# Retention ahead of two mixtures of experts: POOL's mixes and stores of x pinned in the first block alone, and one joined tile of mixed x kept and stored one step later

## Chip, cores and metric

The kernel runs on one core of a Trainium2 chip. The metric is the device time of one execution in microseconds (us), before and after; smaller is better. TensorE (PE) multiplies matrices, VectorE (DVE), ScalarE (ACT) and GpSimd (POOL) work on elements, SyncE (SP) starts most transfers, and POOL starts the stores that this change touches.

## Reference

Three layers run one after the other on 2304 tokens of 512 features: retention (4 batches, 8 heads, 576 positions), a mixture of 4 experts that all run, and a mixture of 8 experts with routing.

```python
def _attn_ref(q, k, v):
    scores = scale * np.matmul(q, k.transpose(0, 1, 3, 2))
    Dmat = np.where(rel >= 0, gamma[:, None, None] ** rel[None, :, :], 0.0)
    return np.matmul(scores * Dmat[None], v)

def _moe_ref(x, domain_probs, w1, w2):
    p = domain_probs / (domain_probs.sum(-1, keepdims=True) + 1e-09)
    for e in range(E):
        out += p[:, e:e + 1] * (np.maximum(x @ w1[e], 0.0) @ w2[e])

def _moe2_ref(x, w_gate, w_output_gate, w1, w2):
    e_idx = np.argmax(x @ w_gate, axis=1)
    # each token through its own expert alone, scaled by its two gates
```

## The kernel before

**Stages.** Retention is cut into 36 steps of 64 positions (`NSTEP`, `NC` = 9 steps to a batch). Four steps (`NS`) make a block of 256 tokens, so there are nine blocks (`NB`). The first mixture starts as soon as the first block of x is there; the steps of the retention are then threaded between its matrix products: `at_hook()` runs one step at a time, at fixed places of the loops over blocks and experts. Steps 0 to 5 run ahead of that in program order. This interleaved stretch lasts until about 175 us of the span; from there on the first mixture goes on alone, and the second follows.

**One step.** `at_step(s)` has PE work out what the state adds (`at_past`, L300), the scores of the next step (`at_scores`, L277), the step's own part (`at_b`, L309) and the new state (`at_state`, L324). All of it lands in one PSUM tile `uo`, of which there is one after the opening. DVE masks the scores (`pf`, L282), adds the state (`sn`) and then reads x out of `uo` into the SBUF tile `xf` of the block (`at_x`, L358). Until it has done so, the next step's L300 cannot write `uo`. `at_parts` then splits the step's x into a high half (ACT, L365) and a low half (POOL, L366), in the tile `xo` (`xc` for blocks 0 and 1). POOL also scales the keys for the state (`ks`, L256), from a tile `vkr` that SP loads.

**Mixed x.** The first mixture multiplies large matrices by a scheme of seven products in place of eight, which needs sums of blocks of x. `x_mix(b, i)` makes them on POOL in place in `xf`, two subtractions at a time, four to a block (L373). `x_keep(b, i)` splits half of the mixed tile: ACT copies the high half (L384), POOL subtracts for the low one (L385). The results go to `xm`, or for blocks 0 and 1 to the upper half of `xc`. `x_store` then writes the tiles to DRAM (`xcd`) by a transfer that POOL starts (L390 and L392).

**Buffers.** `xf` has two buffers, so the first `at_x` of block b+2 (step 4b+8) waits until both keeps of block b have read theirs. `xo` has two. Before the change, mixed x of blocks 2 to 8 lies in two tiles, `xm0` and `xm1`, with one buffer each; a keep of the next block waits for the store of the same half.

**Order.** A scheduler places instructions on each engine. `tc.issue_after(...)` pins an instruction behind another on its own queue; `pace["pool"]` and `pace["act"]` hold the latest such instruction. By `ago(s, b)`, the steps since a block's last one, the kernel before mixes at 1 and 2, keeps at 3 and 4 and stores each half of mixed x at once, pinned.

**Weights.** ACT (L219, L220) and DVE (L221) split the experts' weights into high and low parts, and ACT L487 with DVE L488 mix them. These stand between the instructions of the steps on the same queues. The first mixture's second products are L711 (`po`), its first ones L559 (`ph`).

Of the kernel before, what the change touches and what calls it, by code (L numbers as in the profile page):

```python
# [10 lines left out]
F16 = mybir.dt.float16  # L11
# [12 lines left out]
NSTEP = B * NC  # L24
NT = N // 128
BT = 256
NB = N // BT
# [10 lines left out]
HB = BT // 2  # L38
# [5 lines left out]
BM = 5  # L44
# [100 lines left out]
def kernel(  # L145
# [19 lines left out]
    pe, act, dve, pool, sp = [InOrder(tc, e) for e in (nc.tensor, nc.scalar, nc.vector, nc.gpsimd, nc.sync)]  # L165
# [34 lines left out]
    xcd = dram.tile([NB * 128, 2, 8, 2, HB], F16, name="xcd")  # L200
# [27 lines left out]
    at_1 = at_ctx.enter_context(tc.tile_pool(name="at_1", bufs=3))  # L228
# [3 lines left out]
    qks, raws, pm, st, uos, pace = {}, {}, {}, {}, {}, {}  # L232
    xcs, xfs, xos = {}, {}, {}
# [5 lines left out]
    def load_qk(s):  # L239
        b, c = divmod(s, NC)  # L240
        a = at_raw.tile([128, 10, C], F32, name="qkr", bufs=4)
        pace["sp"] = sp.dma_start(out=a[:, 0:10 if c else 8], in_=qk[b, c][:, 0:10 if c else 8])
        qks[s] = a

    def load_vk(s):
        b, c = divmod(s, NC)
        t = at_raw.tile([128, 10, D], F32, name="vkr")
        pace["sp"] = sp.dma_start(out=t[:, 0:4 if c == NC - 1 else 10], in_=vk[b, c][:, 0:4 if c == NC - 1 else 10])
        raws[s] = (t,)

    def at_split(s):

        ks = None
        if s % NC < NC - 1:
            ks = at_1.tile([128, 4, D], F32, name="ks")
            pool.tensor_tensor(  # L256
                out=ks, in0=raws[s][0][:, 4:8], in1=cst("ktab", 4, 1).to_broadcast([128, 4, D]), op=ALU.mult
            )
        raws[s] += (ks,)
# [25 lines left out]
    def at_open(s):  # L285
        uos[s] = [at_ps[-1].tile([128, 2, 512], F32, tag="uo", name="uo"), set(), None]
# [88 lines left out]
    def x_keep(b, i):  # L375
        m = xfs[b]
        if xos[b][1] is None:
            xos[b][1] = [at_1.tile([128, 2, 2, 2, HB], F16, name="xm" + str(h), bufs=1) for h in range(2)]
        with tc.issue_after(pace["act"].ins):
            if isinstance(xos[b][1], list):  # L380
                hi, lo = [xos[b][1][i][:, a] for a in range(2)]
            else:
                hi, lo = [xos[b][1][:, a, 2 * i:2 * i + 2] for a in range(2)]
            act.activation(out=hi, in_=m[:, i], func=ACTF.Copy)  # L384
            pool.tensor_tensor(out=lo, in0=m[:, i], in1=hi, op=ALU.subtract)  # L385

    def x_store(b, i):
        dst = xcd[b * 128:(b + 1) * 128]
        if i < 2:
            pace["pool"] = pool.dma_start(out=dst[:, :, 4 * i:4 * i + 4], in_=xos[b][i])  # L390
        else:
            pace["pool"] = pool.dma_start(out=dst[:, :, 2 * i:2 * i + 2], in_=xos[b][1][i - 2])  # L392

    def at_step(s):

# [784 lines left out]
    def later_step(s):  # L1180
# [11 lines left out]
        out=p_sb, in0=p_sb, scalar=SO1, in1=ps_inv.to_broadcast([128, NT, E1]), op0=ALU.mult, op1=ALU.mult  # L1192
# [16 lines left out]
    pe, act, dve, pool, sp = nc.tensor, nc.scalar, nc.vector, nc.gpsimd, nc.sync  # L1209
# [4 lines left out]
    def others():  # L1214
        with tc.issue_after(pace["sp"].ins):
            sp.dma_start(out=wgr, in_=wg)
            sp.dma_start(out=kb, in_=cb)
            sp.dma_start(out=k16, in_=c16)

    def gate_split():  # L1220
        with tc.issue_after(pace["act"].ins), tc.issue_after(pace["dve"].ins):
            split(wgr, wg_sb[:, 0], wg_sb[:, 1], S_G)
# [9 lines left out]

    def at_hook():
        s = nxt[0]
        if s >= NSTEP + 4:
            return
        nxt[0] += 1
        if s + 4 < NSTEP:
            load_vk(s + 4)
        if s + 3 < NSTEP:  # L1240
            load_qk(s + 3)
        if NS + 2 < s < NSTEP - 2:
            at_split(s + 2)
        if s == 4 * NS:
            others()
        if s == 6 * NS:
            gate_split()
        if s == NS + 2:
            with tc.issue_after(pace["pe"].ins), tc.issue_after(pace["pool"].ins):
                at_split(s + 2)  # L1250
                at_open(s)
                at_scores(s)
                at_state(s, s, 4 * C)
                at_sum(s, s, 4 * C)
        for b in range(NB):
            if ago(s, b) == 1:
                with tc.issue_after(pace["pool"].ins):
                    x_mix(b, 0)
        if s < NSTEP:
            at_step(s)  # L1260
        for b in range(NB):
            n = ago(s, b)
            if n == 2:
                with tc.issue_after(pace["pool"].ins):
                    x_store(b, 0)
                x_mix(b, 1)
            if 2 < n < 5:
                x_keep(b, n - 3)
                if b > 1:
                    with tc.issue_after(pace["pool"].ins):  # L1270
                        x_store(b, n - 1)
            if b < 2 and n == 5:
                x_store(b, 1)
        if s == NSTEP + 3:
            at_ctx.close()
            wm["b"] = ctx.enter_context(tc.tile_pool(name="w_b", bufs=1)).tile([128, 6, 2048], F16, name="wm_b")
            later["raw"] = ctx.enter_context(tc.tile_pool(name="raw_s", bufs=3))
            later["s16"] = ctx.enter_context(tc.tile_pool(name="s16", bufs=4))
            later["pool"] = ctx.enter_context(tc.tile_pool(name="later", bufs=2))
            later["mix"] = mix_ctx.enter_context(tc.tile_pool(name="mix_ps", bufs=1, space=PSUM))  # L1280
# [107 lines left out]
    for e in range(E1):  # L1388
        for b in range(NB + (e == E1 - 1)):
            last = b == NB  # L1390
            if e == 0 and b <= BM:
                a = [lambda b=b, j=j: l1_first(b, j) for j in range(4)] if 0 < b < BM else l1_mixed(0, b) if b else []
                d = b - (b >= BM)
                c = [] if b == BM - 1 else [lambda d=d, i=i, h=h: l2(d, i, h) for h in range(2) for i in range(2)]
                units = a + c
                if b == BM:
                    units = [a[0], c[0], a[1], a[2], c[1], a[3], c[2], a[4], a[5], c[3], a[6]]
            else:
                a = [] if last else l1_mixed(e, b)
                c = l2_mixed(*prev) if prev else []  # L1400
                units = [f for n in range(7) for f in ([a[n]] if a else []) + ([c[n]] if c else [])]
            if (e, b) == (E1 - 1, 1):
                c_ctx.close()
                open_routing()
                gp.append(ctx.enter_context(tc.tile_pool(name="gp", bufs=2)))
            for u, unit in enumerate(units):
                unit()
                z_from(e == 0 and b < BM and (b == 0 or u >= 4))
                if e == 0:
                    if u == 1 and b >= 2 or (b, u) == (1, 5):  # L1410
                        with tc.issue_after(pace["sp"].ins):
                            x_load((b + 1) % NB, sp, base=b + 1 < BM)
                elif (e, b) == (1, 0):
                    if u == 0:
                        x_load(1, sp)
                elif u == 0 and not last and (e, b) != (E1 - 1, NB - 1):
                    with tc.issue_after(pace["pool"].ins):
                        x_load((b + 1) % NB, pool)
                if e == 0:
                    for _ in range(1 + (b == 0 and u % 2)):  # L1420
                        at_hook()
                if not last:
                    w_plan(e, b, u)
                    s_plan(e, b, u)
                if e == E1 - 1:
                    for g in gate_at.pop((b, u), ()):
                        g()
                    if gate:
                        gate.pop(0)()
            if e == E1 - 1:  # L1430
                if b:
                    gate_plan(b - 1)
                if b == NB - 1:
                    while s_at[0] <= n_stage + 2 or pend_store:
                        s_hook()
                    m_open_x()
                    lane_load(0, 1, early_row[0])
                    for s in range(EARLY):
                        m_x(s, early[5], s, TE * 128)
                if last:  # L1440
                    m_open()
            if e or b >= BM:
                prev = (e, b)
# [112 lines left out]
```

## Time and profile before

| | before |
|---|---|
| median of three runs | 1006.8 us (1004.93 to 1008.66) |
| profiled execution | 1005.25 us, span 1003.5 us |
| granted PE clock, mean | 0.994 of full |
| PE busy in the span | 961.8 us (96%) |
| weight loads, DVE, ACT, POOL busy | 826.3, 573.6, 535.6, 420.9 us |

The span reaches from the first to the last instruction; the execution's own time has 1.75 us more. PE's idle time is what a change of order can give back or add to. The page's row of 40 slices has PE below full only in the first seven (to about 175 us) and in the last one.

### The profile page before, as it was taken

Reading aid. Unit: us, or ns where it says so; the run is one execution under the profiler, and the core shown is the slowest. Engines: PE = TensorE matmul, PEld = TensorE weight load, DVE = VectorE, ACT = ScalarE, POOL = GpSimd, SP = SyncE. Lnnn points to the kernel's source line nnn. Section 1 sums busy time; section 2 is a strip of 40 time slices with the busy share of each in tenths; the row PEclk is TensorE's granted clock in tenths of the full one; section 3 lists DMA queues with packets and bytes.
Section 4 is the critical chain, followed back from the end, with each engine's and each line's share of the span. In section 5 each row is a group of like instructions: output and inputs, shape, how many; then the busy total and the mean of one; then the engine's idle time right before and its main releaser. Section 6 shows DMA issues by size and latency. Waiting matters only on the chain. (4 is left out here: it accounts for less than half of the span.)

```text
span 1003.5 us, 31925 instructions
## 1 busy us (share of the span) xinstructions
PE 961.8 (96%) x13507; PEld 826.3 (82%) x13507; DVE 573.6 (57%) x1290; ACT 535.6 (53%) x1019; POOL 420.9 (42%) x446
## 2 busy tenths in 40 slices
PE   6988899999999999999999999999999999999994
PEld 6565476899999999999999999999987677777773
DVE  5664472466767777766777676888888211211210
ACT  4354353567758777766777676676643122221211
POOL 4686665555546234555343464343223222112111
PEclk9999999999999999999999999999999999999998
DMA  9697875336466777556668726978835616554690
GB/s 351 215 352 236 289 242 183 115 101 200 153 197 177 250 266 235 174 184 198 220 195 297 272 71 160 264 211 227 230 121 203 232 43 229 217 205 158 256 391 32
DMA packets 96051, 209.48 MB, mean 209 GB/s; under 512 B 21598, under 2 KB 42334, under 8 KB 93600
## 3 DMA queue, kind: packets, MB, share of 16 engines
q1 hardware_dynamic: 82784, 159.20, 47.8%
q0 software_dynamic: 13120, 48.20, 15.0%
q8 instruction: 108, 1.77, 0.7%
q14 instruction: 39, 0.32, 0.1%
HBM read 197.88 MB, written 52.99 MB: 250 GB/s over the span
## 5 line engine op out<-in xcount | busy, mean ns | idle before, releaser
L672 PEld LDWEIGHTS <-op 128*128 128x128 f16 x2604 | 245.7, 98 | 26.0 <-POOL s L211 0.6
L606 POOL TENSOR_TENSOR op<-sm,op 128x512 f16<-128x512 f32 x124 | 142.3, 1158 | 226.2 <-ACT op L605 226.1
L587 PEld LDWEIGHTS <-wm_a 128*128 128x128 f16 x3264 | 192.9, 98 | 3.8
L587 PE MATMUL ph<-xc,wm_a 128*128 128x128 f16 x2112 | 132.2, 219 | 0.0
L605 ACT ACTIVATE op<-sm 128x512 f16<-128x512 f32 x124 | 77.5, 634 | 86.3 <-DVE sm L610 84.8
L1094 DVE SCALAR_TENSOR_TENSOR h_s<-p_h,h_s 128x512 f16<-128x512 f32 x40 | 27.6, 691 | 159.1 <-ACT h_s L1093 151.4
L1101 PE MATMUL p_y<-wm_a,h_s 128*128 128x512 f16 x480 | 107.2, 379 | 0.5 <-DVE h_s L1094 0.5
L672 PE MATMUL pv<-wm_a,op 128*128 128x256 f16 x792 | 97.4, 273 | 0.0
L672 PE MATMUL px<-wm_a,op 128*128 128x256 f16 x744 | 91.3, 272 | 0.7 <-DVE acc L680 0.7
L1101 PEld LDWEIGHTS <-h_s 128*128 128x128 f16 x480 | 46.6, 98 | 52.4 <-DVE h_s L1094 0.7
L221 DVE TENSOR_TENSOR s<-pz,s 128x512 f16<-128x512 f32 x111 | 73.9, 682 | 15.9 <-ACT s L220 15.9
L1104 POOL DMA_INDIRECT out_dram<-y_s,sidxm x17 | 17.3, 1019 | 146.3 <-ACT y_s L1103 137.7
L587 PEld LDWEIGHTS <-wm_b 128*128 128x128 f16 x1296 | 76.9, 98 | 1.4
L219 ACT ACTIVATE pz<-sr 128x512 f32<-128x512 f32 x111 | 65.6, 605 | 15.1 <-DVE rk L830 9.1
L490 POOL TENSOR_TENSOR wr<-wr 128x512 f32<-128x512 f32 x48 | 60.5, 1272 | 29.8 <-ACT pz L219 29.1
L1093 ACT ACTIVATE h_s<-p_h 128x512 f16<-128x512 f32 x40 | 23.9, 597 | 78.9 <-PE p_h L1084 74.9
L220 ACT ACTIVATE s<-pz 128x512 f16<-128x512 f32 x111 | 64.0, 599 | 0.6
L221 DVE TENSOR_TENSOR wm_a<-pz,wm_a 128x512 f16<-128x512 f32 x62 | 42.0, 688 | 37.7 <-ACT wm_a L220 37.3
L1103 ACT ACTIVATE y_s<-p_y,x_g 128x512 f32<-128x512 f32 x20 | 13.7, 687 | 92.8 <-PE p_y L1101 83.7
L680 DVE SCALAR_TENSOR_TENSOR acc<-px,p_sb,acc 128x256 f32<-128x256 f32 x124 | 59.1, 476 | 6.7 <-PE px L672 6.5
L1084 PEld LDWEIGHTS <-wm_b 128*128 128x128 f16 x1056 | 60.0, 98 | 2.8 <-issue 0.6
L1084 PE MATMUL p_h<-x_s,wm_b 128*128 128x128 f16 x1056 | 61.6, 219 | 0.3 <-issue 0.2
(231 smaller groups left out, 1809.4 us busy)
## 6 DMA issues: line engine op xcount, KB each, us to landing
wm_a<-w2d SPq DMA_DIRECT2D x20, 2048.0 KB, 8.8
wr<-in_w_dram SPq DMA_DIRECT2D x40, 512.0 KB, 7.9
wm_b<-w1d SPq DMA_DIRECT2D x10, 2048.0 KB
wm_a<-w1d SPq DMA_DIRECT2D x10, 2048.0 KB
sr<-in_w1s_dram SPq DMA_DIRECT2D x64, 256.0 KB, 4.3
w1d<-s SPq DMA_DIRECT2D x64, 256.0 KB, 4.9
sr<-in_w2s_dram SPq DMA_DIRECT2D x64, 256.0 KB, 5.0
w2d<-s SPq DMA_DIRECT2D x64, 256.0 KB, 5.2
```

What stands on the lines that cost most here:

```text
L219: act.activation(out=z, in_=raw, func=ACTF.Copy, scale=scale)
L220: act.activation(out=hi, in_=z, func=ACTF.Copy)
L221: dve.tensor_tensor(out=lo, in0=z, in1=hi, op=ALU.subtract)
L490: pace["pool"] = pool.tensor_tensor(out=quarter(e, n, k, to), in0=quarter(e, n, k, x), in1=quarter(e, n, k, y), op=op)
L587: pe.matmul(bank[:, i], lhsT=w[:, k, u, 128 * i:128 * i + 128], rhs=x[:, v, d, k], start=(first and i == 0 and n == 0), stop=(n == 5), ski ...
L605: act.activation(out=hi, in_=s, func=ACTF.Copy)
L606: pool.tensor_tensor(out=lo, in0=s, in1=hi, op=ALU.subtract)
L672: pe.matmul(out, lhsT=o[a][:, v, k], rhs=w[c][:, k, u], start=(first and n == 0), stop=(n == 11), skip_group_check=True,)
L680: step = dve.scalar_tensor_tensor(out=a, in0=src, scalar=p_sb[:, b * TB + i, e:e + 1], in1=a, op0=ALU.mult, op1=ALU.add)
L1084: pe.matmul(ph[:, j], lhsT=w[k][:, x, f * 128:(f + 1) * 128], rhs=xs[:, y, k], start=(n == 0), stop=(n == 3 * KD - 1),)
L1094: dve.scalar_tensor_tensor(out=lo, in0=ph, scalar=0.0, in1=hi, op0=ALU.max, op1=ALU.subtract)
L1101: pe.matmul(po, lhsT=h[:, a, k], rhs=w[k][:, b], start=(n == 0), stop=(n == 3 * KF - 1))
```

## The change

The changed kernel keeps mixed x in one tile `xm` (one buffer, twice the size) and stores it by one transfer of 512 KB. A block's mixes and first store are pinned behind POOL's last paced instruction for block 0 only; in the other blocks the scheduler places them. Keeps are one step later (4 and 5 steps ago), and so is the store of mixed x, one for a block at 6 steps (5 for the last block). Since the last steps then reach one further, one unit of block 4 runs two hooks.

```diff
@@ x_keep, x_store
         if xos[b][1] is None:
-            xos[b][1] = [at_1.tile([128, 2, 2, 2, HB], F16, name="xm" + str(h), bufs=1) for h in range(2)]
+            xos[b][1] = at_1.tile([128, 2, 4, 2, HB], F16, name="xm", bufs=1)
         with tc.issue_after(pace["act"].ins):
-            if isinstance(xos[b][1], list):
-                hi, lo = [xos[b][1][i][:, a] for a in range(2)]
-            else:
-                hi, lo = [xos[b][1][:, a, 2 * i:2 * i + 2] for a in range(2)]
+            hi, lo = [xos[b][1][:, a, 2 * i:2 * i + 2] for a in range(2)]
             act.activation(out=hi, in_=m[:, i], func=ACTF.Copy)
             pool.tensor_tensor(out=lo, in0=m[:, i], in1=hi, op=ALU.subtract)
 
     def x_store(b, i):
-        dst = xcd[b * 128:(b + 1) * 128]
-        if i < 2:
-            pace["pool"] = pool.dma_start(out=dst[:, :, 4 * i:4 * i + 4], in_=xos[b][i])
-        else:
-            pace["pool"] = pool.dma_start(out=dst[:, :, 2 * i:2 * i + 2], in_=xos[b][1][i - 2])
+        pace["pool"] = pool.dma_start(out=xcd[b * 128:(b + 1) * 128, :, 4 * i:4 * i + 4], in_=xos[b][i])
@@ at_hook
-        if s >= NSTEP + 4:
+        if s >= NSTEP + 5:
             return
             if ago(s, b) == 1:
-                with tc.issue_after(pace["pool"].ins):
+                with ExitStack() as pins:
+                    if b == 0:
+                        pins.enter_context(tc.issue_after(pace["pool"].ins))
                     x_mix(b, 0)
             n = ago(s, b)
             if n == 2:
-                with tc.issue_after(pace["pool"].ins):
-                    x_store(b, 0)
+                x_store(b, 0)
                 x_mix(b, 1)
-            if 2 < n < 5:
-                x_keep(b, n - 3)
-                if b > 1:
-                    with tc.issue_after(pace["pool"].ins):
-                        x_store(b, n - 1)
-            if b < 2 and n == 5:
+            if 3 < n < 6:
+                x_keep(b, n - 4)
+            if n == (6 if b < NB - 1 else 5):
                 x_store(b, 1)
-        if s == NSTEP + 3:
+        if s == NSTEP + 4:
@@ where the hooks are called
-                    for _ in range(1 + (b == 0 and u % 2)):
+                    for _ in range(1 + (b == 0 and u % 2 or (b, u) == (BM - 1, 3))):
                         at_hook()
```

The order of PE, DVE and SP is the same in both kernels; POOL's and ACT's change. The changed file is seven lines shorter, so its keeps are L381 (ACT) and L382 (POOL), its stores L385, its L480 is L487 of before and its L538 is L545.

**POOL between block 1's mixes and block 2's.** First the kernel before: the two keeps of block 1 (`xc<-xf`) follow its mixes, then come its store, the next steps' `ks` and parts, and block 2's four mixes.

```order
L385 TENSOR_TENSOR xc<-xf,xc 128x512 x2
L390 DMA xcd<-xc 256x1x1024
L256 TENSOR_TENSOR ks<-vkr,ka 128x256
L366 TENSOR_TENSOR xo<-xf,xo 128x4x64
L390 DMA xcd<-xc 256x1x1024
L256 TENSOR_TENSOR ks<-vkr,ka 128x256
L366 TENSOR_TENSOR xo<-xf,xo 128x4x64
L256 TENSOR_TENSOR ks<-vkr,ka 128x256
L366 TENSOR_TENSOR xo<-xf,xo 128x4x64
L373 TENSOR_TENSOR xf<-xf 128x256 x4
```

The same place after the change, from the first keep of block 1 on:

```order
L382 TENSOR_TENSOR xc<-xf,xc 128x512
L256 TENSOR_TENSOR ks<-vkr,ka 128x256
L366 TENSOR_TENSOR xo<-xf,xo 128x4x64
L256 TENSOR_TENSOR ks<-vkr,ka 128x256
L366 TENSOR_TENSOR xo<-xf,xo 128x4x64
L256 TENSOR_TENSOR ks<-vkr,ka 128x256
L373 TENSOR_TENSOR xf<-xf 128x256
L366 TENSOR_TENSOR xo<-xf,xo 128x4x64
L373 TENSOR_TENSOR xf<-xf 128x256
L385 DMA xcd<-xo 256x1x1024
L382 TENSOR_TENSOR xc<-xf,xc 128x512
L373 TENSOR_TENSOR xf<-xf 128x256
```

The second keep of block 1 has moved behind three `ks` (of steps 13, 14 and 15), three parts, two mixes of block 2 and the store of block 2's own x; two stores of `xc` no longer stand in this stretch (one went ahead into the opening, one comes after it). DVE's `at_x` of step 12, block 3's first, now waits for that second keep.

**ACT between the weight splits of the stretch at 75 to 83 us.** Before, both keeps of block 3 (the tiles `xm_1616` and `xm_1617`) stand here, around the parts of step 16 and one half of a weight split.

```order
L219 ACTIVATE pz<-wr 128x512
L384 ACTIVATE xm_1616<-xf 128x512
L365 ACTIVATE xo<-xf 128x4x64
L220 ACTIVATE wm_a<-pz 128x512
L384 ACTIVATE xm_1617<-xf 128x512
L219 ACTIVATE pz<-wr 128x512
L220 ACTIVATE wm_a<-pz 128x512
L365 ACTIVATE xo<-xf 128x4x64
```

After the change, the same place:

```order
L219 ACTIVATE pz<-wr 128x512
L220 ACTIVATE wm_a<-pz 128x512
L365 ACTIVATE xo<-xf 128x4x64
L381 ACTIVATE xm<-xf 128x512
L219 ACTIVATE pz<-wr 128x512
L220 ACTIVATE wm_a<-pz 128x512
L365 ACTIVATE xo<-xf 128x4x64
```

One keep is left ahead of the last split, the first of block 3; the split before it no longer stands behind a keep. The second keep has gone three parts further on.

**POOL at the end of the interleaved stretch.** Before, block 8's four mixes are followed by its two keeps with a half-store behind each.

```order
L373 TENSOR_TENSOR xf<-xf 128x256
L390 DMA xcd<-xo 256x1x1024
L373 TENSOR_TENSOR xf<-xf 128x256 x3
L385 TENSOR_TENSOR xm_2978<-xf,xm_2978 128x512
L392 DMA xcd<-xm_2978 256x1x512
L385 TENSOR_TENSOR xm_2979<-xf,xm_2979 128x512
L392 DMA xcd<-xm_2979 256x1x512
```

After the change:

```order
L373 TENSOR_TENSOR xf<-xf 128x256
L385 DMA xcd<-xo 256x1x1024
L373 TENSOR_TENSOR xf<-xf 128x256 x2
L382 TENSOR_TENSOR xm<-xf,xm 128x512
L385 DMA xcd<-xm 256x1x1024
L382 TENSOR_TENSOR xm<-xf,xm 128x512 x2
L385 DMA xcd<-xm 256x1x1024
```

The second keep and the store of block 7 now stand behind block 8's mixes, and block 8's keeps, which write the same tile, follow that store.

## Rows read from the trace of the kernel before

**Rows 1.** Windows: the interleaved stretch, one piece of it, and the 25 us behind it.

```profile
50.00:175.00 125.00, 110.44 (x2071) 78.58 (x2072) 65.67 (x181) 59.37 (x117) 84.85 (x117) 0.99 0.77 260
120.00:125.00 5.00, 5.00 (x60) 2.08 (x53) 1.68 (x4) 1.33 (x4) 3.03 (x5) 0.66 0.92 306
175.00:200.00 25.00, 25.00 (x306) 20.27 (x304) 10.03 (x17) 13.60 (x25) 13.05 (x11) 1.00 0.41 123
```

**Rows 2.** Waits of PE from 50 to 175 us: total, times, longest.

```profile
PE uo L300 <- DVE xf L358: 6.3, 4, 3.7
PE sc L277 <- DVE pf L282: 3.9, 2, 3.2
...
PE sc L277 <- DMA qkr<-in_qk_dram: 0.8, 1, 0.8
```

**Rows 3.** Timeline around 81 to 84 us: POOL, ACT, PE (start, duration, idle before).

```profile
73.93 0.68 POOL L392 DMA_DIRECT2D xcd<-xm  x1
...
78.41 0.63 ACT L384 ACTIVATE xm<-xf 128x512 f16<-128x512 f32 x1 [2.40 <-POOL xf L373]
...
81.63 0.63 ACT L384 ACTIVATE xm<-xf 128x512 f16<-128x512 f32 x1 [1.79 <-DMA xcd<-xm]
...
84.48 0.46 PE L277 MATMUL sc<-qkr 64*64 64x64 f32 x16 [3.19 <-DVE pf L282]
```

**Rows 4.** Timeline around 115 to 119 us: ACT and PE.

```profile
114.53 0.63 ACT L384 ACTIVATE xm<-xf 128x512 f16<-128x512 f32 x1 [6.31 <-POOL xf L373]
116.47 0.63 ACT L384 ACTIVATE xm<-xf 128x512 f16<-128x512 f32 x1 [1.31 <-DMA xcd<-xm]
...
119.33 0.46 PE L300 MATMUL uo<-qkr,sn 64*64 64x64 f32 x16 [3.69 <-DVE xf L358]
```

**Rows 5.** Timeline around 149 to 155 us: ACT and PE.

```profile
149.46 0.63 ACT L384 ACTIVATE xm<-xf 128x512 f16<-128x512 f32 x1 [2.31 <-POOL xf L373]
...
155.22 0.46 PE L300 MATMUL uo<-qkr,sn 64*64 64x64 f32 x16 [1.81 <-DVE xf L358]
```

**Rows 6.** Timeline from 51 to 62 us: POOL, then `at_x` of step 12, then PE.

```profile
51.70 2.27 POOL L385 TENSOR_TENSOR xc<-xf,xc 128x512 f16<-128x512 f32 x2
54.27 0.68 POOL L390 DMA_DIRECT2D xcd<-xc  x1 [0.30 <-POOL xc L385]
...
60.49 0.61 POOL L256 TENSOR_TENSOR ks<-vkr,ka 128x256 f32<-128x256 f32 x1 [2.36 <-DMA vkr<-in_vk_dram]
61.06 0.68 POOL L366 TENSOR_TENSOR xo<-xf,xo 128x256 f16<-128x256 f32 x1
61.70 2.35 POOL L373 TENSOR_TENSOR xf<-xf 128x256 f32<-128x256 f32 x3
...
58.55 0.41 DVE L358 TENSOR_TENSOR xf<-uo,ka 128x256 f32<-128x256 f32 x1
...
60.91 0.40 PE L300 MATMUL uo<-qkr,sn 64*64 64x64 f32 x11 [0.69 <-issue]
```

**Rows 7.** Transfers from 44 to 62 us: sum, and POOL's stores (count, size, landing).

```profile
DMA packets 2128, 6.40 MB, mean 356 GB/s; under 512 B 224, under 2 KB 224, under 8 KB 2123
...
xcd<-xc POOLq DMA_DIRECT2D x4, 512.0 KB, 8.0
```

**Rows 8.** Transfers from 0 to 190 us: POOL's stores (count, size, median landing).

```profile
xcd<-xo POOLq DMA_DIRECT2D x7, 512.0 KB, 5.1
xcd<-xm POOLq DMA_DIRECT2D x14, 256.0 KB, 4.5
```

**Rows 9.** Timeline around 126 to 131 us: POOL's `ks` of step 27, `at_x` of step 28.

```profile
125.86 0.60 POOL L256 TENSOR_TENSOR ks<-vkr,ka 128x256 f32<-128x256 f32 x1 [2.11 <-PE uo L324]
...
131.43 0.41 DVE L358 TENSOR_TENSOR xf<-uo,ka 128x256 f32<-128x256 f32 x1
```

**Rows 10.** Timeline around 172 to 177 us: POOL's last store of the stretch, ACT's next wait.

```profile
172.74 0.68 POOL L392 DMA_DIRECT2D xcd<-xm  x1 [0.30 <-POOL xm L385]
...
177.22 0.60 ACT L628 ACTIVATE s<-pq 128x512 f32<-128x512 f32 x1 [4.99 <-DMA xcd<-xm]
```

## Prediction

> **What bounds the kernel now.** I read the page's row of slices first: PE is full from about 175 us to the last slice, so the change can act only in the interleaved stretch ahead of that. The windows say how much is at stake there. Of the 125 us from 50 to 175, PE is busy 110.44, so 14.56 us are idle, and in the next 25 us it is busy throughout [rows 1]. No order of POOL's work can give back more than that (what comes ahead of 50 us belongs to loads and the opening, which the change touches in one store alone). Next, the waits of PE in that stretch: 6.3 us go to L300, which waits for DVE's `at_x` to empty `uo`, and 3.9 to L277, which waits for DVE's mask; both times DVE is the last to come [rows 2]. The timeline then shows what made DVE late in the three large cases.
> Gap A (PE idle 3.19 us until 84.48): ACT's second keep of block 3 waits 1.79 us for the landing of the store of the same half of block 2, begun at 73.93 and landed 7.7 us later. Behind that keep stand the split of a weight on ACT and DVE, then the mask, then PE [rows 3].
> Gap B (3.69 us until 119.33): the same at block 5, with 1.31 us of wait for a landing [rows 4].
> Gap C (1.81 us until 155.22): ACT waits 2.31 us for block 7's mixes, and two keeps stand among the splits that DVE needs [rows 5].
> So POOL, busy 42% of the span, sets the end of three waits through what stands behind it on ACT and DVE.
>
> **The change part by part.** Sizes are against the profiled execution, 1005.25 us, which lies 1.55 us below the median of the runs, 1006.8.
>
> *The new wait, at step 12.* The order has `at_x` of step 12 behind the second keep of block 1, and that keep behind the `ks` of step 15. Before, the keeps ended near 54 us and `at_x` ran at 58.55, unhindered. The `ks` of step 15 waited for its load until 60.49 [rows 6]. From the start of that `ks` to the end of the keep stand, with the rows' durations: `ks` 0.61, two mixes at 2.35/3 = 0.78 each, parts 0.68, the issue of a store 0.68, the keep 2.27/2 = 1.14. That makes 4.67 us. When can that `ks` start? Its load is slow in a stretch in which 6.40 MB move at 356 GB/s and four stores of `xc` are out [rows 7]; two of these, 1 MB, leave the stretch. At 356 GB/s that MB takes 2.9 us. If three quarters of it stood ahead of the load, 2.2 us, `ks` starts at 58.3, the keep ends at 63.0, `at_x` runs to 63.4 and L300 goes at 63.45. Before, it went on at 60.91 [rows 6]: 2.5 us lost. Bounds: with the load as late as before, the keep ends at 65.2 and L300 goes 4.7 us later. With a load that lands in time, POOL's own queue decides: 58.3 was already the time at which POOL fell idle before (60.49 less 2.36, 58.1), and one keep and two store issues (1.14 + 2 x 0.68 = 2.5) no longer stand ahead of it, so `ks` could start at 55.6 to 56.3, the keep would end by 61.0, L300 go at 61.45, and 0.55 be lost. I take the middle, +2.5, since the stretch is full of transfers and loses one MB of 6.4. On DVE the state of step 13 and its mask stand behind the waiting `at_x`, and PE waits with them, since `uo` has one buffer.
>
> *Less traffic at 44 to 60 us.* The same MB may also shorten the 0.8 us that PE waits for a `qkr` load [rows 2]: -0.5, from 0 to -0.8.
>
> *One store in place of two.* Seven transfers of 512 KB replace 14 of 256 KB. The rows have 5.1 us for a 512 KB store of x and 4.5 for the halves [rows 8], but 7.7 for the half-store that ends gap A, and 8.0 for 512 KB in the fullest stretch [rows 3, 7]. A keep needs the tile of the block before. It used to wait for half a block's store, now for the whole; against that, only one keep is left ahead of the weight split in gaps A and B, where before two were, the second of them late.
> In gap A the joined store stands behind both of block 2's keeps, as the second half did, so it starts about where that did, and the first keep of block 3 ends where the second did, if the landing is the same 7.7: nothing gained. It gains 1.4 if the landing is short, since then the mixes of block 3 decide: they ended at 78.41 and will end about two parts or stores later, near 80.2, against 81.63 [rows 3]. It loses 0.6 if 512 KB take longer by 5.1 - 4.5. I take 0.
> Gap B is the same case: from -1.3 (the wait for the landing gone) to +0.6, taken as 0 [rows 4].
> What hides the moved keep of each block (0.63 us of ACT, 1.14 of POOL) is POOL's idle time, and ACT's, outside the gaps.
> The Trainium skill bears on this on its page "DMA: Bandwidth & Descriptors", in the section on the anatomy of one DMA on the SWDGE path: about 2.0 us for each transfer plus its bytes over 436 GB/s. By it, an estimate, 256 KB take 2.6 us and 512 KB 3.2, and every keep would find its tile free; the sum would be about 2.7 us lower. The rows here have 4.5 and 5.1, so the fixed part is larger, but the step between the sizes, 0.6, agrees.
>
> *Gap C.* One weight split comes ahead of block 7's first keep in the new order, so the splits that DVE waits for have one keep (0.63) less in front; ACT's wait of 2.31 stays, since the mixes are POOL's [rows 5]. I take -0.9, from -1.8 (all of it) to +0.6 (mixes later by one parts).
>
> *Other first steps.* Steps 20 and 28 wait for keeps in the same way. At 28: `ks` of step 27 starts at 125.86; 4.67 us later is 130.5, and `at_x` ran at 131.43: 0.9 us to spare [rows 9]. I take 0, up to +1.5 if POOL is late by more than that.
>
> *End of the stretch.* Block 8's keeps write the tile that block 7's store reads, and that store comes last but one: two landings in a row. The last store began at 172.74 and ACT waited for it until 177.22 [rows 10]. Now it begins near 174.5 and lands near 179.5, 2.2 us later. PE has work through 200 us [rows 1], which covers this; without the cover, up to +2. I take 0.
>
> *Pins, hook.* Pins on one queue cost nothing by themselves; the order they leave is counted above. The second hook of block 4 only has step 40 run in the same unit.
>
> *Sum.* 2.5 - 0.5 + 0 + 0 - 0.9 + 0 + 0 = +1.1 us: 1006.35 on the scale of the profiled execution, and 1007.9 on that of the median. I predict 1008.0.
>
> **The rivals.** 0.5% of the time, 5 us, is about what a measurement of this kernel can tell from no change.
> *Slower: step 12's wait at its upper bound.* The load of step 15 lands no earlier, +4.7. A long idle time of PE can also cost clock: behind gap B's 3.69 us the granted clock of the next 5 us was 0.66, which at 5 x 0.34 is 1.7 us [rows 1, 4]. With the long landings in gaps A and B (+0.6 each) that is +7.6: 1012.9, or 1014.4 by the median. It decides when `ks` of step 15 starts after about 59.1 (3.3 lost there, which with the clock's 1.7 makes 5) and gap C gives nothing back. For it: transfers fill that stretch. Against it: 1 MB leaves the stretch.
> *Faster: the joined store takes the waits out of the gaps.* If 512 KB land in the 5.1 us of the stores of x, A gives 1.4, B 1.3 and with it the clock's fall, 1.7, C 1.8, the `qkr` load 0.8, and step 12 costs 0.55: -6.45, so 998.8, or 1000.4 by the median. It decides at landings of at most about 6 us at 74 and 110 us, together with step 15's load landing before 56.5. For it: the median row. Against it: 7.7 us in gap A for half the bytes.
> The page's section of rules for kernel authors, in the Trainium skill ("DMA: Bandwidth & Descriptors"), asks for one large transfer in place of many small ones; that would bring this case. The page "Perfetto Trace Analysis", section on DMA optimizations, says that split transfers let some work start sooner where the DMA engines idle, which speaks for the halves. No row above favours either strongly.
> *No change: nothing of it reaches PE.* Step 12 loses its lower bound, 0.55, and the landings are as before: 1005.8, or 1007.3. For it: POOL idles 58% of the span.
>
> **How the numbers follow.** Chances: forecast 0.38, nothing reaches PE 0.25, slower 0.25, faster 0.12. The first two lie within 0.5%. The range for eight in ten takes in the forecast with its bounds and most of the slower case, and cuts the far half of the faster: 1002 to 1014.5; the forecast's own range is 1004.5 to 1011.
>
> **What would show it.** In the changed profile: `at_x` of step 12 idle behind POOL's keep of block 1, with L300 after it near 63.5 (right) or at 61 (the wait was hidden); the first keep of blocks 3 and 5 on ACT released by a landing of `xcd<-xm` near 81 and 116; gap C shorter by about 1 us; ACT's L628 near 179.5 and PE still full from 175 us. The prediction falls if idle time of PE from 50 to 175 us comes out below 10 us or above 19, or if a first `at_x` of another block (16, 20, 24, 28) stalls PE by more than 1.5 us.

## The result and the profile after

| | before | after |
|---|---|---|
| median of 10 runs each | 1006.95 us (1004.56 to 1011.62) | 1012.98 us (1009.27 to 1016.91) |
| ratio to before, 95% interval | | 1.0062 (1.0041 to 1.0083) |
| profiled execution, span | 1005.25 us, 1003.5 us | 1012.54 us, 1010.6 us |
| granted clock, mean | 0.994 | 0.989 |
| PE busy, 13507 products in both | 961.8 us | 967.4 us |

The change costs about 6 us. The forecast was 1008.0, a little over the time before. The time lies in the range for eight in ten, 1002 to 1014.5, but outside the forecast's own range, 1004.5 to 1011; it lies near the rival that prices the wait at step 12 at its upper bound, 1014.4.

The windows of the changed kernel that answer to [rows 1], and the pieces of it in which the clock is low:

```profile
50.00:175.00 125.00, 108.60 (x2056) 76.38 (x2054) 65.34 (x181) 56.66 (x112) 78.86 (x110) 0.95 0.73 245
65.00:70.00 5.00, 3.18 (x70) 2.72 (x71) 3.38 (x10) 1.91 (x4) 4.48 (x7) 0.72 0.67 216
90.00:95.00 5.00, 2.88 (x51) 1.92 (x52) 3.08 (x10) 1.92 (x4) 2.92 (x4) 0.61 0.29 95
95.00:100.00 5.00, 5.00 (x78) 2.51 (x77) 0.86 (x4) 1.10 (x2) 0.84 (x2) 0.71 0.14 52
175.00:200.00 25.00, 25.00 (x277) 18.85 (x276) 6.82 (x11) 11.52 (x21) 9.01 (x10) 1.00 0.51 165
```

The idle time of PE from 50 to 175 us is 125 - 108.60 = 16.40 us, against 14.56. By these two profiles that is far less than the loss, and most of the rest is busy time: the granted clock is 0.95 in this stretch against 0.99, and in the whole span the same 13507 products keep PE busy 967.4 us against 961.8. A second profile of the kernel before, shown with **before_again** below, divides the loss otherwise. The waits of PE in the same stretch, in answer to [rows 2]:

```profile
PE uo L300 <- DVE xf L358: 7.9, 4, 4.3
PE sc L277 <- DVE pf L282: 4.8, 2, 4.1
```

The two longest are new or longer: 4.3 us on `at_x`, 4.1 on the mask. The first is the wait at step 12. The timeline there has POOL, then DVE, then PE, in answer to [rows 6]:

```profile
61.69 0.61 POOL L256 TENSOR_TENSOR ks<-vkr,ka 128x256 f32<-128x256 f32 x1 [2.62 <-DMA vkr<-in_vk_dram]
62.26 0.72 POOL L373 TENSOR_TENSOR xf<-xf 128x256 f32<-128x256 f32 x1
62.95 0.67 POOL L366 TENSOR_TENSOR xo<-xf,xo 128x256 f16<-128x256 f32 x1
63.69 0.72 POOL L373 TENSOR_TENSOR xf<-xf 128x256 f32<-128x256 f32 x1
64.36 0.68 POOL L385 DMA_DIRECT2D xcd<-xo  x1
64.99 1.23 POOL L382 TENSOR_TENSOR xc<-xf,xc 128x512 f16<-128x512 f32 x1
...
66.25 0.42 DVE L358 TENSOR_TENSOR xf<-uo,ka 128x256 f32<-128x256 f32 x1 [4.58 <-POOL xc L382]
...
66.82 0.72 PE L300 MATMUL uo<-qkr,sn 64*64 64x64 f32 x13 [4.34 <-DVE xf L358]
```

Read it from the bottom: PE waits for `at_x`, `at_x` for the second keep of block 1, and that keep stands behind the parts, mixes and store that follow the `ks` of step 15, which waits for a load. The 65 to 70 us window behind it has the clock at 0.72. Before, the same window had it full:

```profile
65.00:70.00 5.00, 4.75 (x136) 4.09 (x140) 3.20 (x10) 2.80 (x7) 4.50 (x7) 1.00 0.77 242
```

The second place is block 3, in answer to [rows 3]: POOL's joined store of block 2, ACT's first keep of block 3, and PE.

```profile
80.46 0.68 POOL L385 DMA_DIRECT2D xcd<-xm  x1 [0.30 <-POOL xm L382]
...
82.39 0.78 POOL L385 DMA_DIRECT2D xcd<-xo  x1
...
89.21 0.63 ACT L381 ACTIVATE xm<-xf 128x512 f16<-128x512 f32 x1 [4.91 <-DMA xcd<-xm]
...
92.07 0.70 PE L277 MATMUL sc<-qkr 64*64 64x64 f32 x16 [4.12 <-DVE pf L282]
```

The joined store lands 8.7 us after its start; before, the half-store had 7.7. The store of block 3's own x begins 1.9 us behind it, where before it came only after the gap. At block 5 PE waits less than before [rows 4], and at block 7 as well [rows 5]:

```profile
125.86 0.63 ACT L381 ACTIVATE xm<-xf 128x512 f16<-128x512 f32 x1 [6.64 <-DMA xcd<-xm]
...
128.73 0.71 PE L300 MATMUL uo<-qkr,sn 64*64 64x64 f32 x16 [2.32 <-DVE xf L358]
...
163.87 0.46 PE L300 MATMUL uo<-qkr,sn 64*64 64x64 f32 x16 [0.85 <-DVE xf L358]
```

A ledger by steps shows where time went and came back. Each number is the end of the last L309 of that step on PE's timeline, in us.

| step | before | before, second profile | after | early keeps of blocks 0, 1 | with filler too |
|---|---|---|---|---|---|
| 12 | 57.01 | 57.22 | 59.52 | 58.61 | 57.77 |
| 14 | 66.35 | 67.56 | 73.35 | 68.10 | 66.85 |
| 16 | 73.97 | 75.22 | 80.95 | 75.70 | 74.45 |
| 19 | 89.48 | 93.03 | 99.48 | 94.78 | 90.19 |
| 25 | 112.94 | 116.49 | 123.71 | 119.58 | 115.54 |
| 27 | 125.50 | 127.57 | 134.71 | 129.19 | 128.03 |
| 35 | 159.47 | 161.55 | 168.12 | 163.93 | 160.58 |

From step 12 to 14 the change takes 13.83 us against 9.34 and 10.34. From 16 to 19 it takes 18.53 against 15.51 and 17.81: here the two profiles of the kernel before differ by 2.3 us, and the second shows why, below. From 25 to 27 the change takes 11.00 against 12.56 and 11.08. From step 12 to step 35 it takes 108.60 us in all, against 102.46 and 104.32.

The 2.5 us by which it is late at step 12 already are not the work of its new order. The fourth `xc<-xf` of POOL in the opening starts at 24.22 us, against 21.39 before, and the first instruction that the change moves there, a store of `xc`, comes only at 25.97. The experiment before_filler below has the order of the kernel before on POOL and ACT and differs from it on PE only from step 17 on, and it ended step 12 at 58.83, 1.8 us late. So the opening differs by that much from one execution to the next.

### The profile page after: what moved, and what is told of

Same layout as the page of the kernel before. It is cut to its first block, busy times and chain, and to the rows that moved or that the text cites. A ratio compares the mean times of both kernels' runs of the same rounds, so it can differ in the third digit from the quotient of the medians.

```text
span 1010.6 us, 31914 instructions
## 1 busy us (share of the span) xinstructions
PE 967.4 (96%) x13507; PEld 830.7 (82%) x13507; DVE 574.7 (57%) x1290; ACT 535.6 (53%) x1019; POOL 415.5 (41%) x439
```

## The experiments

Theory: the loss is two waits, at step 12 and at block 3, each with a fall of the clock behind it. Rival 1: the wait at step 12 is all of it. Rival 2: the freed mixes and stores are the cause. All ratios are to the kernel before, with 95% intervals.

**early_keep_b01.** One part undone: the keeps of blocks 0 and 1 one step earlier again. On POOL only the stretch from block 1's keeps to block 2's mixes changes.

```diff
-            if 3 < n < 6:
-                x_keep(b, n - 4)
+            k = 4 if b > 1 else 3
+            if k <= n < k + 2:
+                x_keep(b, n - k)
```

> The changed kernel, with the keeps of blocks 0 and 1 alone back at 3 and 4 steps. Theory (two waits and the clock's fall behind each make the loss): the 4.3 us wait of PE at step 12 goes, and with it the fall of the clock at 65 to 70 us; the wait of about 4 us at the first keep of block 3 stays, with its fall. About 5.4 us less than the changed kernel: near 1007.6. Rival 1 (the wait at step 12 is the whole loss): 6 us less, equal to the kernel before, and the clock stays full at block 3 too. Rival 2 (the freed mixes and stores are the loss): 1011 or more.

1008.08 us, 1.0019 (1.0000 to 1.0038). So 0.43% of the 0.62% goes with the wait at step 12; steps 12 to 14 take 9.49 us again. What is left is hardly told from nothing, so by the time alone rival 1 isn't excluded. Block 3 keeps its wait (5.11 us) and its low clock:

```profile
87.30 0.70 PE L277 MATMUL sc<-qkr 64*64 64x64 f32 x16 [5.11 <-DVE pf L282]
...
85.00:90.00 5.00, 2.65 (x51) 1.83 (x52) 2.85 (x9) 2.15 (x5) 3.00 (x4) 0.65 0.37 131
90.00:95.00 5.00, 5.00 (x76) 2.33 (x75) 0.82 (x3) 1.10 (x2) 0.67 (x1) 0.67 0.17 59
```

**block1_keeps_late.** The same part alone, put into the kernel before.

```diff
-            if 2 < n < 5:
-                x_keep(b, n - 3)
+            k = 4 if b == 1 else 3
+            if k <= n < k + 2:
+                x_keep(b, n - k)
...
-            if b < 2 and n == 5:
+            if b < 2 and n == (6 if b else 5):
```

> The kernel before, with the keeps of block 1 alone one step later (and its store with them): the second one then stands behind the ks of step 15 and three mixes of block 2, as in the changed kernel, and nothing else of the change is in. Theory (the wait of step 12 is the largest part of the loss): PE waits 4 to 5 us at step 12 with DVE's at_x behind POOL's keep, and the clock falls behind it: 4 to 6 us slower than before, 1011 to 1013. Rival (the loss needs the rest of the change): within 2 us of before.

1012.91 us, 1.0040 (1.0017 to 1.0062). Added alone it costs what undoing it gives back. POOL, DVE and PE show the same chain, and the clock falls behind it:

```profile
65.21 1.15 POOL L385 TENSOR_TENSOR xc<-xf,xc 128x512 f16<-128x512 f32 x1
...
66.40 0.42 DVE L358 TENSOR_TENSOR xf<-uo,ka 128x256 f32<-128x256 f32 x1 [5.73 <-POOL xc L385]
...
66.97 0.72 PE L300 MATMUL uo<-qkr,sn 64*64 64x64 f32 x13 [4.96 <-DVE xf L358]
...
65.00:70.00 5.00, 3.03 (x69) 2.69 (x70) 3.23 (x9) 1.91 (x4) 4.64 (x7) 0.68 0.47 145
```

**before_free_mixes.** The kernel before with pins in block 0 alone.

```diff
-                with tc.issue_after(pace["pool"].ins):
+                with ExitStack() as pins:
+                    if b == 0:
+                        pins.enter_context(tc.issue_after(pace["pool"].ins))
                     x_mix(b, 0)
...
-                with tc.issue_after(pace["pool"].ins):
-                    x_store(b, 0)
+                x_store(b, 0)
```

> The kernel before, with its mixes and first stores pinned in block 0 alone: this part of the change by itself. Theory: the keeps of block 1 stay ahead, no wait at step 12; half-stores as before: within 2 us of the kernel before, 1005 to 1009. Rival 2 (the freed mixes and stores are the loss): 1011 or more.

1009.35 us, 1.0018 (0.9996 to 1.0039): not told from no change, and below the interval of the whole change. Rival 2 falls as the whole cause; a share of up to 0.4% isn't excluded.

**join_alone.** The kernel before with the one tile of the change and one store, begun where the second half-store stood. The keeps keep their steps. The new pin also holds the stores of blocks 0 and 1, so that the last store of `xc` begins at 65.19 us in place of 56.09; no run tells this apart from the join.

```diff
...
             if 2 < n < 5:
                 x_keep(b, n - 3)
-                if b > 1:
-                    with tc.issue_after(pace["pool"].ins):
-                        x_store(b, n - 1)
-            if b < 2 and n == 5:
-                x_store(b, 1)
+            if n == (4 if b > 1 else 5):
+                with tc.issue_after(pace["pool"].ins):
+                    x_store(b, 1)
```

> The kernel before with the joined tile and its one store alone, begun where the second half-store of a block stood, with the keeps at their old steps and all pins left. Theory: block 3's keep waits for 512 KB begun no earlier than before; PE's wait of 3.2 us there grows past 3.7, the clock falls behind it: 2 to 5 us slower than before, 1009 to 1012. Rival (size doesn't matter): within 1.5 us of before.

1007.45 us, 0.9996 (0.9981 to 1.0010). The loss that the theory expected did not come, although the profile has the longer wait at block 3:

```profile
86.04 0.71 PE L277 MATMUL sc<-qkr 64*64 64x64 f32 x16 [4.44 <-DVE pf L282]
```

The explanation came from **before_again**, the kernel before once more.

> The kernel before, unchanged, for a second profile. Theory: the waits of PE stand where they stood; whether the clock falls behind the wait of 3.2 us at block 3 may differ, and then the time with it by about 2 us. Rival: the same granted clock in every window, 1.00 from 80 to 95 us.

1007.82 us. PE waits at block 3 as in the first profile (3.40 us against 3.19), but this time the clock falls behind it, to 0.50 in the next 5 us, which is the lower of its two levels, 1.2 GHz. The first profile had it full there. The fence has the second profile's wait and windows, then the first one's window:

```profile
85.52 0.70 PE L278 MATMUL sc<-qkr 64*64 64x64 f32 x16 [3.40 <-DVE pf L283]
...
85.00:90.00 5.00, 4.43 (x55) 2.51 (x56) 2.74 (x10) 1.41 (x3) 2.83 (x6) 0.50 0.37 104
90.00:95.00 5.00, 5.00 (x88) 3.23 (x87) 1.62 (x6) 1.10 (x2) 1.08 (x2) 0.84 0.55 182
50.00:175.00 125.00, 112.13 (x2092) 79.09 (x2082) 66.62 (x182) 59.34 (x117) 84.86 (x118) 0.96 0.76 256
...
85.00:90.00 5.00, 4.76 (x112) 3.02 (x113) 2.25 (x10) 2.10 (x4) 3.38 (x6) 1.00 0.57 201
```

So the kernel before already pays for a low clock at block 3 in some executions, and the first profile was one without. Against the second, steps 16 to 19 cost the join alone 18.40 - 17.81 = 0.6 us, and the whole change 0.7. Against it the loss divides otherwise too: from 50 to 175 us the clock was 0.96 already, against 0.95 after the change, and PE was idle 125 - 112.13 = 12.87 us, so that the change adds 3.5 us of idle time. The runs speak for this: their mean granted clock is 0.9905 in 28 executions of the kernel before and 0.9886 in the 10 of the changed one. That is 0.2%, about 2 of the 6 us by estimate.

**two_tiles_free.** The changed kernel with early keeps for blocks 0 and 1, and the joining undone: each half stored behind its keep.

```diff
...
-            if 3 < n < 6:
-                x_keep(b, n - 4)
-            if n == (6 if b < NB - 1 else 5):
+            k = 4 if b > 1 else 3
+            if k <= n < k + 2:
+                x_keep(b, n - k)
+                if b > 1:
+                    x_store(b, n - 2)
+            if b < 2 and n == 6:
                 x_store(b, 1)
```

> Early keeps for blocks 0 and 1, as before, and the joining undone: two tiles of mixed x, each stored right behind its keep, with the free mixes and the later keeps of the other blocks left in. Against early keeps alone (1008.1) only the joined tile and store differ. Theory (the landing of the joined store makes the wait at block 3): the first keep of block 3 waits for a half-store begun about 1 us earlier and half as large, so it runs 2 to 4 us earlier, PE's wait of 5.1 us there shrinks to 2 to 3, and the clock stays full: 1003 to 1005.5. Rival (the traffic of that stretch makes the landing late, whatever the size): the wait stays near 5 us, 1007 to 1009.

1006.66 us, 0.9990 (0.9976 to 1.0005). ACT's keep is now released by POOL's mixes, not by a landing, and PE waits 2.24 us in place of 5.11. The first half-store is not only half as large, it also begins 1.3 us earlier than the joined one of early_keep_b01 (74.35 against 75.69); the two aren't separated. The clock fell all the same, against what was expected:

```profile
82.05 0.63 ACT L384 ACTIVATE xm<-xf 128x512 f16<-128x512 f32 x1 [2.52 <-POOL xf L373]
...
84.91 0.46 PE L277 MATMUL sc<-qkr 64*64 64x64 f32 x16 [2.24 <-DVE pf L282]
...
85.00:90.00 5.00, 4.71 (x59) 2.49 (x60) 2.05 (x8) 1.41 (x3) 2.49 (x4) 0.66 0.53 192
```

**filler_at_block3.** Early keeps for blocks 0 and 1, the joined store left in, and extra products on PE ahead of the wait.

```diff
         at_past(s)
+        if s == 17:
+            for _ in range(9):
+                pe.matmul(uos[s][0][:, 0, 256:512], lhsT=cst("xtab", KD * C)[:, 0:128], rhs=cst("xtab", KD * C), start=False, stop=True, skip_group_check=True)
         if s + 1 < NSTEP:
             at_scores(s + 1)
```

> Early keeps for blocks 0 and 1, the joined store left in, and nine extra products of constants (128x256, f32) on PE at step 17, in columns of uo that nothing reads, ahead of the product that waits about 5 us. Theory (the clock falls because PE stands idle): the wait is filled, the clock stays full behind it, and about 2 to 3 us come back: 1005 to 1006.5. Rival (the fall has another cause): the clock falls at 85 to 95 us as before, 1008 or a little more.

1006.04 us, 0.9988 (0.9972 to 1.0003), against 1.0019 without the filler. ACT's keep still waits 4.54 us for the landing, but PE is busy meanwhile (each product stands as two records, one of which is missing) and the clock stays full:

```profile
82.34 0.63 ACT L381 ACTIVATE xm<-xf 128x512 f16<-128x512 f32 x1 [4.54 <-DMA xcd<-xm]
...
77.80 3.83 PE L394 MATMUL uo<-ka 128*128 128x256 f32 x17
...
85.00:90.00 5.00, 4.69 (x109) 2.73 (x112) 2.34 (x9) 2.03 (x4) 1.92 (x3) 1.00 0.30 94
90.00:95.00 5.00, 5.00 (x128) 4.33 (x118) 2.64 (x8) 2.26 (x6) 3.70 (x6) 1.00 0.78 235
```

Steps 16 to 19 take 15.74 us against 19.08, of which 0.85 is an earlier landing (from the end of step 16 to the keep, 7.89 against 8.74 us). So about 2.5 us behind the wait were the clock's, by estimate, and here work on PE kept it up. The mean granted clock of the runs agrees: 0.993, against 0.990 in those of early_keep_b01.

**before_filler** and **two_tiles_filler** put seven and five such products into the kernel before and into two_tiles_free.

> The kernel before, with seven of the same extra products at step 17 (about 3 us), where PE waits 3.2 us. Theory: the wait is filled; in the executions in which the clock falls behind it about 2 us come back, in the others nothing: 1004.5 to 1007. Rival (the products cost their time): 1008 or more.

> Two tiles free, with five extra products at step 17 (about 2.1 us), where PE waited 2.2 us and the clock fell to 0.66. Theory: the clock stays full behind it, about 1.5 us less than two tiles free: 1004 to 1006. Rival: no less, 1006.5 to 1008.

1006.56 us, 0.9994 (0.9973 to 1.0014), and 1007.08 us, 0.9993 (0.9974 to 1.0013). In both profiles the clock is 1.00 from 80 to 95 us, as expected, but neither time is told from the kernel before. The second was expected to be about 1.5 us faster than two_tiles_free, and isn't: 0.9993 against 0.9990.

**store_other_tile** and **both_undone.** The second store of blocks 2 to 8 sends `xo` in place of `xm`, in the changed kernel and with early keeps for blocks 0 and 1. The mixed x of these blocks is left out in DRAM. Its edit is `in_=xos[b][i if b < 2 else 0]`.

> The changed kernel, but the second store of blocks 2 to 8 sends the tile xo again in place of xm: as many bytes, and no keep waits for a landing. It leaves out the mixed x of these blocks in DRAM. Theory: the wait of PE at block 3 falls from 4.1 to about 1 us, the clock stays full there (3.4 us), and block 5 loses about 0.7 to 2.3 us of wait; the wait at step 12 stays. 1003 to 1007. Rival 1 (step 12 is the whole loss): no change, 1011 to 1013. Rival 2 (the freed mixes and stores): no change either.

> Both edits together: early keeps for blocks 0 and 1, and the second store of blocks 2 to 8 sends xo (the mixed x of these blocks is left out in DRAM). Theory: the two gains add, 5.4 and 6 or more: 998 to 1002, below the kernel before, since that one waits for landings as well. Rival 1: as early keeps alone, near 1006.5. Rival 2: 1011 or more.

1039.46 and 1035.47 us. The expected times did not come, and these times say nothing of the keeps: the first mixture reads other values, and so the second gets others to route by. At the end of step 35 store_other_tile is 2.9 us ahead of the changed kernel, and its span is 28 us longer, so the loss lies behind the interleaved stretch. Only that stretch can be read. With store_other_tile, PE's wait at block 3 is 0.41 us, and steps 16 to 19 take 11.89 us against 18.53. With both it is 2.38 us, against 5.11 with early keeps alone, and step 27 ends at 124.09, 1.4 us ahead of the kernel before. So the wait for the landing was what held block 3, nearly all of it in the changed kernel and about half with early keeps.

What was won did not last: from step 28 to 29 they lose 9.02 and 7.70 us, against 3.81 before. The trace of store_other_tile shows the wait of step 12 once more, now at step 28: `at_x` stands behind POOL's late second keep of block 5, and PE behind `at_x`. With both, PE waits 3.37 us there.

```profile
137.12 0.42 DVE L358 TENSOR_TENSOR xf<-uo,ka 128x256 f32<-128x256 f32 x1 [4.61 <-POOL xm L382]
...
137.69 0.71 PE L300 MATMUL uo<-qkr,sn 64*64 64x64 f32 x16 [4.50 <-DVE xf L358]
```

**odd_keeps_late.** The kernel before with the keeps and half-stores of blocks 3, 5 and 7 one step later.

```diff
-            if 2 < n < 5:
-                x_keep(b, n - 3)
+            k = 4 if b > 1 and b % 2 else 3
+            if k <= n < k + 2:
+                x_keep(b, n - k)
                 if b > 1:
                     with tc.issue_after(pace["pool"].ins):
-                        x_store(b, n - 1)
+                        x_store(b, n - k + 2)
```

> The kernel before with its two tiles and pins, and only the keeps and half-stores of blocks 3, 5 and 7 one step later, which gives the stores of blocks 2, 4 and 6 a step more to land. Theory: the waits for landings ahead of DVE's splits (1.8 and 1.3 us) go, and the fall of the clock behind 119 us with them, 3 to 4 us; the second keeps now stand behind the next block's mixes, and the at_x of steps 20 and 28 lose up to 1.5 each: 1003 to 1006.5. Rival (the late second keeps cost as step 12's did): 1008 to 1012.

1007.07 us, 0.9993 (0.9979 to 1.0007). Block 3's wait fell to 1.01 us, and step 27 ended at 122.17, 3.3 us ahead of before. Then the first `at_x` of block 7 stood behind the late second keep of block 5, and it was given back:

```profile
131.79 0.42 DVE L358 TENSOR_TENSOR xf<-uo,ka 128x256 f32<-128x256 f32 x1 [3.53 <-POOL xm L385]
...
132.36 0.46 PE L300 MATMUL uo<-qkr,sn 64*64 64x64 f32 x16 [3.41 <-DVE xf L358]
```

That is the mechanism of step 12 at another block. The time missed the expected 1003 to 1006.5 by a little. No version here is faster than the kernel before beyond its interval.

Of the theory, the wait at step 12 is shown from both sides. Block 3 as a second loss is not: the kernel before waits there too, and in its second profile the clock falls there as well. Joining the store in the freed order may cost up to 0.3% (1.0019 against 0.9990), which the intervals hardly separate.

## Why the prediction was right or wrong, point by point

- **The new wait at step 12.** The mechanism, its place and its chain were as forecast, and two experiments show it from both sides (0.43% undone, 0.40% added). The size failed: the sum had +2.5 us. The step that failed is "if three quarters of it stood ahead of the load", by which `ks` of step 15 would start 2.2 us earlier. Counted from the end of step 12, it started 2.17 us behind (61.69 - 59.52), against 3.48 before (60.49 - 57.01): 1.3 us earlier. The stretch from 44 to 62 us moved 6.09 MB after, against 6.40, so other transfers took most of the place of the MB that left. L300 came 7.30 us behind the end of step 12 against 3.90, which is 3.4 us of wait, the forecast's upper bound of 4.7 less 1.3. The second term that was too small is the clock behind the wait, which the sum put at nothing and left to a rival: the stretch from step 12 to 14 is longer by 4.5 us (13.83 - 9.34) by the first profile of before, by 3.5 by the second.
- **The chain from `ks` to the keep's end**, 4.67 us in the sum, took 66.22 - 61.69 = 4.53. Durations from rows carried over.
- **Less traffic, the `qkr` wait.** The wait for `qkr` of [rows 2] is gone from the six largest, the smallest of which is 0.4 us; -0.5 was about right.
- **One store in place of two.** At block 3 the forecast was 0 with +0.6 at the far end. The store began about at the end of step 16, where the second half-store had begun, as forecast. PE's wait grew by 0.9 to 4.12, and the landing by 1.0 to 8.7. The step left out the store of block 3's own x, which the freed order puts 1.9 us behind the joined one. That this made the landing long is not shown: 512 KB without it landed in 7.1 us (join_alone), the half-store with it 1.3 us behind in 7.4 (before_free_mixes), and at block 3 only both together took more than the 7.7 of before (8.05 to 8.7). Taken alone on the kernel before, the join costs nothing measurable; with the mixes freed and the keeps late, undoing it brings 1.0019 to 0.9990.
- **The figure of the Trainium skill.** The Trainium skill ("DMA: Bandwidth & Descriptors", anatomy of one DMA, SWDGE path) led to an estimate of 3.2 us for 512 KB. The joined store here took 8.7 from issue to landing, so in this stretch the estimate is far too short and the measurement decides.
- **Gaps B and C.** Forecast 0 and -0.9; measured waits 2.32 against 3.69, and 0.85 against 1.81. C's size was right: steps 33 to 34 take 4.71 us against 5.67 in both profiles of before, and ACT's wait for the mixes stayed, at 1.94. B gave 1.6 us by the first profile of before and 0.1 by the second, so 0 stands.
- **Other first steps.** A stall of a block's first `at_x` would show in the step behind it. Steps 16 to 17, 24 to 25 and 28 to 29 take the same in both kernels (3.6, 3.8 and 3.8 us), 20 to 21 takes 4.3 us against 3.8: no stall beyond the bound of 1.5, as forecast. The 0.9 us to spare at step 28 seem to hang on the waits ahead of it: where these were shortened, in store_other_tile, both_undone and odd_keeps_late, PE waits 4.50, 3.37 and 3.41 us there.
- **End of the stretch.** The last store began at 182.50, which is 14.4 us behind step 35 against 13.3 before, 1.1 later (forecast 1.8), and PE stayed full from 175 to 200 us: the cover held.
- **The chances.** The forecast of little change had 0.38, the slower rival 0.25. The time came out near that rival's 1014.4, but its parts did not: the load did come earlier, the wait was 3.4 us and not 4.7, and gap C gave back what the rival denied it. That the range held the time is in part luck: the sum of the steps gave +1.1 us, where 6 were measured.

From the end of step 35 to the end of the span the change won back 1.5 us of its 8.65 in the profile; where was not followed up, and what makes up the last 0.19% stays open.

## What to carry to other kernels

Moving work off a busy place is only safe if one asks which buffer it frees: a keep that reads a two-buffered tile sets when the block after next may begin, and one step later put it behind a load, two mixes and a store. When several instructions on an in-order engine follow one that waits for a load, the last of them inherits that wait, and so does the engine that waits for it. In a kernel whose PE is full for most of its span, price an added wait with the slow products behind it too, and take a second profile of the kernel before: one execution with a lucky clock or opening makes a change look worse, and puts the loss down to the wrong thing.

## What the runs showed that was not expected

- The kernel before has the clock full behind a wait of 3.19 us in one profile and at 0.50 for 5 us behind one of 3.40 in another; two_tiles_free had 0.66 behind 2.24 us. The length of the last wait alone doesn't decide.
- Extra products of constants, 3.83 us of them, in a wait of PE cost nothing that the time shows and kept the clock at 1.00 where it had been 0.65 and 0.67.
- A store of 512 KB that another 512 KB follows 1.9 us later took 8.7 us to land. The half-store of 256 KB without one had taken 7.7, and 512 KB without one took 7.1 in join_alone: twice the bytes alone did not lengthen it.
- Two kernels with the same order up to step 17 ended step 12 at 57.01 and 58.83 us.
